# Attention beside a long convolution on one core: the first load in two halves, a filter reversal and a last turn placed later, and VectorE blocks to a later step

## Chip, cores, metric

The kernel runs on one core of one Trainium2 chip. The metric is device time in microseconds (us) of one execution; lower is better. The kernel before took 864.2 us in the median of five runs (860.75, 861.68, 864.2, 867.88, 868.1). The profiled execution took 860.75 us, and its span, from the first to the last instruction, is 859.0 us.

## The reference

Two independent results lie side by side in the output, 512 columns each, for 2048 tokens, all in bf16.

```python
# A: multi-head attention, H = 32 heads of Dh = 16
qkv = (x @ wqkv) -> q, k, v            # x: 2048 x 512
scores = q k^T * Dh ** -0.5            # no mask
a = softmax(scores) v @ wo
# B: short shift, gate, long causal convolution, gate
k_shift[s] = sum_t k[s - 3 + t] * shift_k[:, 3 - t]   # 4 taps a channel
kv = k_shift * v
y = irfft(rfft(kv) * rfft(ssm_k))[:S] + kv * ssm_D    # 2048 taps a channel
b = B_q * y
out = concat([a, b], -1)
```

## The kernel before, in words

**Attention.** The 32 heads are handled four at a time: a block is one head's scores for 128 keys against 512 queries, a 128 x 512 tile in one PSUM bank. There are 4 query quarters x 8 groups x 16 key tiles x 4 heads = 2048 blocks. A group has two passes of four heads; the even and odd heads of a 32-row strip are told apart by two masked copies of the queries, `par` 0 and 1, which VectorE writes as it takes the projected queries out of PSUM (L377, for the first ones L469). Blocks are gathered in steps, `T` = 0 to 740. A step takes two or three banks (`banks_of`, L477 to L484): `emit_qk` issues its score matmuls (L536), ScalarE takes the exponential of the whole step in one instruction (L547), and two steps later `pv_step` and `emit_pv` multiply with the values (L629), accumulating in one bank for the group. At the end of a group VectorE transposes the sums (L693), takes reciprocals (L700), normalises (L704) and transposes back (L715); then the output projection follows (`op_mm`, L746). The last `2 * N_TAIL` blocks go in steps of two, so that the third bank of each set is free for the output projection of the last query quarter (`tail_mm`, `tail_banks`, L1014 to L1019, starting at step NT - 9 = 732).

**VectorE's share of the exponentials.** From step 56 on, `dve_block` may take one block of a three-bank step away from ScalarE. `exp_on_dve` works it out in five VectorE instructions (L583, three of L590, L595). It is allowed when the planned backlog of VectorE is under 3.9 us, and only for T < NT - N_TAIL - GAP = 741 - 9 - 7 = 725 (L557).

**Convolution.** The filter `ssm_k` is loaded as rows (`KZN`), reversed in time by VectorE in four instructions (`kz_turn`, L423), gets `ssm_D` added (`kz_store`, L428), and is stored to a scratch tensor in HBM (L429). From there 512 loads of 512 KB, each a Toeplitz matrix of one channel, stream back through 12 rows of `WR` on SP's queue for the whole run (`load_wr`, L784). `conv_lags` multiplies them with the gated `KV` (L801), with output in the bank `BGB`. After four quads of channels VectorE copies the bank to `YB` (L816); after eight, `conv_turn` transposes `YB` on TensorE (L827) and VectorE multiplies with `B_q` into `QN` (L836). After 64 quads GpSimd's queue stores `QN` to the output.

**What sets the order.** The order is written out when the program is built. A planner keeps a modelled clock for each engine (`Eng.op`, with a duration `us` for each operation) and for the DMAs (`dma`), and places work by it. Each engine then runs its list strictly in order with the semaphore waits that the list implies. VectorE's work that isn't urgent waits in streams (`flow`); `advance` takes from them when the modelled VectorE has time, the stream whose start is earliest first, subject to each piece's `gate`. The four reversals and the store are such pieces (`piece`, L440 to L443), with no gate: they were placed where the model let the filter land. `emit_bg` places the convolution in the room that TensorE has in a step, and the last `conv_turn` as soon as all quads are through (L960 to L963). After it, `keep_busy` issues a spare matmul in each step until 732.

**The start.** SP's queue loads `x` by transposing DMAs, 512 tokens each (`load_x`, L269), then the filter in two halves, `ssm_D`, the rest of `x` and the values of B. ScalarE's queue loads the first 128 columns of the query weights, of the key weights, and then the other weights (L272 to L278). TensorE runs 12 matmuls on zeros (`warm`, L446 to L451), makes the masks (L457), and projects the first queries (L463, 512 tokens in bank 6) and the first 256 keys (L465, bank 7), alternating over the four slices of the contraction. VectorE takes the queries out in two instructions, one for each `par` (L469); ScalarE takes the keys out (L471). Then step 0 begins.

**The end.** `op_mm(qb, 3, 0, 3)` adds three parts of the last output tile; the fourth part of each of the four tiles (L1041) waits for the last group's transposes; VectorE and ScalarE take the tiles out in turn (L766, L764), and SP's and ScalarE's queues store them.

Of the kernel before, what the change touches and what calls it, by code (L numbers as in the profile page):

```python
# [5 lines left out]
ACT = mybir.ActivationFunctionType  # L6
ALU = mybir.AluOpType
# [32 lines left out]
KEYS0 = 256  # L40
# [11 lines left out]
FIX_HI = 2.0 ** 15 - 256.0  # L52
A3, A2, A1 = 255023.64843928182, 77186915383.44943, -6435437372016724.0
A4 = 9.315941845433171e-20
N_TAIL = 9
R_FX = 4
R_EH = 2
R_PTD = 5
T_DVE = 56
T_SLOT = 190  # L60
SLOT = 21
N_SLOT = 25
GAP = 7
AHEAD = 4
BACKLOG = 3.9
MARGIN = 0.35
SPARE = 0.1
# [8 lines left out]
V512 = (0.60, 0.726)  # L76
# [55 lines left out]
def bass_concat_heads__mha_block__ssm_conv_h3__prompt_kernel(  # L132
# [21 lines left out]
    def sem(name):  # L154
        return enter(nc.semaphore(name))
# [5 lines left out]
    xT = sb("xT", [128, 4, S])  # L161
# [30 lines left out]
    WO = WV  # L192
# [16 lines left out]
    def at(*deps):  # L209
        return pe.at(deps)  # L210
# [41 lines left out]
        return dve.op(fn, deps, us=us)  # L252

    d_w = [DmaSem(sem(f"d_w{i}")) for i in range(5)]
    d_x = [DmaSem(sem(f"d_x{i}")) for i in range(4)]
    d_kv = [DmaSem(sem(f"d_kv{i}")) for i in range(6)]
    d_tap, d_kz, d_kzw, d_wo = [DmaSem(sem(n)) for n in ("d_tap", "d_kz", "d_kzw", "d_wo")]
    d_q = [DmaSem(sem(f"d_q{i}")) for i in range(2)]
# [9 lines left out]
    def load_x(sc):  # L268
        h = dma(sp, d_x[sc], xT[:, :, sc * 512:(sc + 1) * 512], x2[sc * 512:(sc + 1) * 512, :], transpose=True)  # L269
        h_x[sc] = [h]  # L270
    load_x(0)
    h_wq = [dma(act, d_w[0], WQ[:, :, 0:128], wview[:, :, 0:128], kb=128)]  # L272
    h_wk = [dma(act, d_w[1], WK[:, :, 0:128], wview[:, :, D:D + 128], kb=128)]
    h_wv = dma(act, d_w[2], WV, wview[:, :, 2 * D:3 * D])
# [142 lines left out]
    def piece(make, deps, us=V512, gate=lambda: True):  # L417
        early_dve.append(("k", deps, make, us, gate))

    def kz_turn(c, us):  # L420
        rev = KZN[c // 2][:, c % 2, :]
        rev = bass.AP(tensor=rev.tensor, offset=KZN[c // 2][:, c % 2, S - 1:S].offset, ap=[rev.ap[0], [-1, S]])
        h_kzt[0] = dve.op(lambda e: e.tensor_copy(KZS[:, c, 0:S], rev), [h_kzl], us=us)  # L423
        if c == 3:
            load_kt(0, h_kzt[0])
# [13 lines left out]

    piece(make_dg, lambda: [], (0.0, 0.0))  # L440
    for c in (2, 3, 0, 1):
        piece(lambda us, c=c: kz_turn(c, us), lambda: [h_kzl])
    piece(kz_store, lambda: [h_kzt[0]], (0.1, 0.22))  # L443


    def warm(e):  # L446
        ins = None
        for _ in range(12):
            ins = e.matmul(PS[:, 0, :], lhsT=PT[:, 0, 0:128], rhs=PT[:, 0, 0:512], start=True, stop=True)
        return ins  # L450
    pe.op(warm, [h_w0], us=(4.0, 4.0))  # L451


    def spread(e):
        ins = None
# [2 lines left out]
        return ins  # L458
    h_mask = pe.op(spread, [h_pat], us=(0.2, 0.3))
    h_mask = bank_free[1] = dve.op(lambda e: e.tensor_scalar(MASK[:, :], PS[:, 1, 0:2], QSCALE, None, ALU.mult), [h_mask])  # L460
    for dc in range(4):
        last_dc = {"start": dc == 0, "stop": dc == 3}
        h = pe.op(lambda e, dc=dc, kw=last_dc: e.matmul(PS[:, 6, :], lhsT=WQ[:, dc, 0:128], rhs=xT[:, dc, 0:512], **kw),  # L463
                  [h_x[0][0], h_wq[0]], us=(0.215, 0.345), run=0.213)
        hk = pe.op(lambda e, dc=dc, kw=last_dc: e.matmul(PS[:, 7, 0:KEYS0], lhsT=WK[:, dc, 0:128], rhs=xT[:, dc, 0:KEYS0], **kw),  # L465
                   [h_x[0][0], h_wk[0]], us=(0.11, 0.24), run=0.107)
    for par in range(2):
        h_q[(0, par)] = bank_free[6] = dve.op(
            lambda e, par=par: e.tensor_scalar(QT[:, 0, par, :], PS[:, 6, :], MASK[:, par:par + 1], None, ALU.mult),  # L469
            [h, h_mask], us=V512)  # L470
    h_k0 = bank_free[7] = act.op(lambda e: e.activation(KTo[:, 0, 0:KEYS0], PS[:, 7, 0:KEYS0], ACT.Copy), [hk], us=(0.28, 0.42))  # L471


    NBLK = NQB * NG * KT * 4
# [79 lines left out]
            exp_on_dve(bl[n], banks[n], h)  # L554

    def dve_block(T):
        if len(banks_of[T]) < 3 or T < T_DVE or T >= NT - N_TAIL - GAP:  # L557
            return None
        i = len(on_dve)
        if i >= R_FX and i - R_FX not in h_last:  # L560
            return None
        todo = sum(us[0] for f in flow for _, _, _, us, _ in f)
        if max(dve.t - pe.t, 0.0) + todo > BACKLOG:
            return None
        n = blk_group(queue[2])
        if len([b for b in queue if blk_group(b) == n]) - 3 >= 2.6 * GAP:
            return queue[2]
        n += 1
        ahead = [b for b in queue if blk_group(b) == n]
        if len(ahead) < 4 * KT - AHEAD + 1 or (n // NG, n % NG) not in h_q or (n % NG // 2, 0) not in h_k:  # L570
            return None
        return ahead[0]
# [166 lines left out]
    def op_mm(qb, t, o0, o1, bank):  # L739
        dd = [bank_free[bank] if o0 == 0 else None, h_wop[0]]  # L740
        dd += [h_otn[(4 * qb + o, t + 1)] if qb == NQB - 1 and o == 3 else h_otn[4 * qb + o] for o in range(o0, o1)]

        def fn(e):
            ins = None
            for o in range(o0, o1):
                ins = e.matmul(PS[:, bank, :], lhsT=OTN[:, (4 * qb + o) % R_O, t * 128:(t + 1) * 128], rhs=WO[:, o, :],  # L746
                               start=(o == 0), stop=(o == 3))
            return ins
        return pe.op(fn, dd, us=(0.105 + 0.215 * (o1 - o0), 0.235 + 0.216 * (o1 - o0)),
                     run=0.213 * (o1 - o0))  # L750
# [70 lines left out]
    def conv_turn(b, bank):  # L821
        pbf = PS[:, bank, :].bitcast(BF16)

        def fn(e):
            ins = None
            for k in range(8):
                ins = e.transpose(pbf[:, 128 * k:128 * k + 128], YB[:, k // 4, 128 * (k % 4):128 * (k % 4) + 128],  # L827
                                  IDN[:, :])
            return ins
        h = pe.op(fn, [bank_free[bank], h_ybw[0], h_idn], us=(0.54, 0.681), run=0.43)  # L830
        h_yb[0] = h
        sl = b // 8
        yv = pbf.rearrange("p (c j) -> p c j", j=32)[:, :, 0:NB].rearrange("p c j -> p j c")
        yv = bass.AP(tensor=yv.tensor, offset=pbf[:, NB - 1:NB].offset, ap=[yv.ap[0], [-1, NB], [32, CHB]])
        qv = QN[:, :, CHB * (b % 8):CHB * (b % 8) + CHB]
        hh = urgent(lambda e: e.tensor_tensor(qv, yv, qv, ALU.mult), [h, h_qn[sl]], slack=0.3, us=V512)  # L836
        bank_free[bank] = hh
        if b % 8 == 7:
            dst = out2[:, D + 256 * sl:D + 256 * (sl + 1)].rearrange("(t p) c -> p t c", p=128)
            ho = dma(pool, d_outB[0], dst, QN[:, :, :], [hh])  # L840
            if sl == 0:
                load_qn(1, [ho])
# [100 lines left out]
    def emit_bg(T):  # L943
        st = state
        unit_step(T)
        if T == N_EARLY:
            assert not early and not part[0]
            load_wop(pe_last())
        if not st["started"] and kv_n[0] == 4:
            st["started"] = True  # L950
        if T in tail_mm:
            assert st["qd"] == C // 4 and not st["turn"], (T, st)
            for t, g in tail_mm[T]:
                op_mm(NQB - 1, t, g, g + 1, tail_banks[t])
            return
        if st["qd"] == C // 4 and not st["turn"] and st["op"] == len(later_op):
            if T < min(tail_mm):
                bank_free[BGB] = pe.op(keep_busy, [bank_free[BGB]])
            return
        if st["turn"] and st["qd"] == C // 4:  # L960
            conv_turn(C // 32 - 1, BGB)
            st["turn"] = False
            return  # L963
        if not st["started"]:
            return
        left_us = max(1.14 * (NT - END - T), 1.0)
        st["lags"] = min(st["lags"] + min(PACE * st["left"] / left_us, RATE) * (pe.t - st["t"]), CAP)
        st["t"] = pe.t
        left = min(LAGS, int(st["lags"]), int((room(T) - 0.06) / 0.055))
        while left > 0 and st["qd"] < wr_next[0] and kv_n[st["qd"] // 32] == 4 and at(h_wr[st["qd"]]) + WAIT <= pe.t:  # L970
            if st["turn"] and st["qd"] % 4 == 3 and st["lag"] + left >= NB:
                left = NB - 1 - st["lag"]
                if left <= 0:
                    break
            n0 = st["lag"]
            if n0 == 0 and st["qd"] % 4 == 0 and at(bank_free[BGB]) > pe.t - 0.2:
                break
            n1 = min(n0 + left, NB)
            left -= n1 - n0
            st["lags"] -= n1 - n0  # L980
            st["left"] -= n1 - n0
            conv_lags(st["qd"], n0, n1)
            st["lag"] = n1 % NB
            if n1 == NB:
                st["qd"] += 1
                if st["qd"] % 4 == 0:
                    st["turn"] = st["turn"] or st["qd"] % 8 == 0
                    break
# [48 lines left out]

    qb = NQB - 1
    op_mm(qb, 3, 0, 3, tail_banks[3])
    for t in range(4):  # L1040
        h = op_mm(qb, t, 3, 4, tail_banks[t])  # L1041
        op_out_end(qb, t, tail_banks[t], h)
# [54 lines left out]
```

## Time and profile before

| what | number |
|---|---|
| median of five runs | 864.2 us |
| profiled execution | 860.75 us |
| its span | 859.0 us |
| ScalarE busy | 837.5 us, 97% |
| VectorE busy | 780.8 us, 91% |
| TensorE busy | 739.2 us, 86% |
| ScalarE's exponentials (L547) | 741 instructions |
| blocks on VectorE (L583) | 212 |
| DMA engines, share of queue q1 | 86.1% |

Read it so: "busy" is time in which the engine has an instruction at work, "idle before" the time that it had none before an instruction of that group, with the instruction or transfer that ended the wait. A time with an `L` is the line of the kernel. A timeline row gives start, duration, engine, line, operation, output and input, count, and in brackets the idle time before it and its releaser; a row of several instructions gives the time from the first's start to the last's end. `SPq` and `ACTq` are the queues on which DMAs are issued, and the duration of such a row is that of the issue, not of the transfer.

### The profile page before, as it was taken

The numbers are of one execution on the slowest core, as the hardware profiler recorded it, in microseconds if no ns is written. First come the engines' busy times: TensorE is split into PE (matmuls) and PEld (weight loads), VectorE is DVE, ScalarE is ACT, GpSimd is POOL, SyncE is SP. The second block draws the span as 40 slices with busy tenths as digits, with TensorE's granted clock in tenths as the row PEclk, the third lists the DMA queues.
The fourth block names the chain that finished last, engine by engine and source line by source line (L and its number), as shares of the span: only waits on it lengthen the run. The fifth ranks groups of instructions, "written<-read, shape, count | busy, mean of one in ns | idle before, by whom it ended". The sixth has DMA issues, their size and how long they took to land.

```text
span 859.0 us, 29408 instructions
## 1 busy us (share of the span) xinstructions
PE 739.2 (86%) x13180; PEld 301.4 (35%) x13180; DVE 780.8 (91%) x1325; ACT 837.5 (97%) x746; POOL 17.3 (2%) x33
## 2 busy tenths in 40 slices
PE   7988999999888888888888888888888888888877
PEld 2222343443333333333333333333333333333332
DVE  3228999999999999999999999999999999999992
ACT  6999999999999999999999999999999999999997
POOL 2000000000000000000000000000000000000000
PEclk9999999999999999999999999999999999999998
DMA  9960059779999999999999999999999999999942
GB/s 271 263 231 2 1 190 334 254 258 320 408 408 407 386 407 393 400 406 404 393 395 376 360 397 388 398 370 397 407 408 394 385 403 409 407 408 393 403 168 71
DMA packets 104813, 289.36 MB, mean 337 GB/s; under 512 B 35184, under 2 KB 37232, under 8 KB 104304
## 3 DMA queue, kind: packets, MB, share of 16 engines
q1 hardware_dynamic: 99424, 279.35, 86.1%
q0 software_dynamic: 1808, 6.29, 2.2%
q10 hardware_dynamic: 3456, 1.84, 0.8%
q8 instruction: 104, 1.70, 0.8%
q14 instruction: 21, 0.17, 0.1%
HBM read 276.83 MB, written 6.42 MB: 330 GB/s over the span
## 4 chain that ended last, share of the span: by engine, by line
ACT 62%; DMA 14%; DVE 12%; PE 7%; SPq 3%; issue 1%; ACTq 0%
ACT PT L547 62%; DMA WR<-kz_scratch 14%; DVE EH L590 5%; PE PS L536 3%; SPq L220 3%; DVE FX L583 2%; DVE PTD L595 2%; PE PS L801 1%; PE PS L629 1%; DMA WR<-in_B_ssm_D_dram 1%; DVE QT L377 1%; PE PS L746 0%; DVE YB L816 0%; DVE DT L693 0%; PE PS L827 0%
## 5 line engine op out<-in xcount | busy, mean ns | idle before, releaser
L547 ACT ACTIVATE PT<-PS 128x1536 bf16<-128x1536 f32 (+1 forms) x741 | 834.5, 1352 | 8.4 <-PE PS L536 7.5
L536 PE MATMUL PS<-QT,KTo 32*128 32x512 bf16 x2048 | 302.2, 385 | 88.4 <-ACT PT L547 72.5
L590 DVE SCALAR_TENSOR_TENSOR EH<-EH,FX 128x512 f32<-128x512 f32 x424 | 283.7, 687 | 0.1
L801 PE MATMUL PS<-WR,KV 128*5 128x128 bf16 (+15 forms) x8192 | 221.7, 220 | 13.6 <-DMA WR<-kz_scratch 12.5
L629 PE MATMUL PS<-PT,VAF 128*32 128x512 bf16 x1836 | 201.1, 391 | 4.6 <-DVE DT L693 2.8
L801 PEld LDWEIGHTS PS<-WR,KV 128*2 128x2 bf16 (+15 forms) x8192 | 148.9, 87 | 96.5 <-issue 37.9
L536 PEld LDWEIGHTS PS<-QT,KTo 32*128 32x128 bf16 x2048 | 72.8, 91 | 266.4 <-ACT PT L547 231.8
L583 DVE TENSOR_SCALAR FX<-PS 128x512 f32<-128x512 f32 x212 | 146.4, 690 | 6.3 <-PE PS L536 5.8
L595 DVE SCALAR_TENSOR_TENSOR PTD<-EH,FX 128x512 uint16<-128x512 f32 x212 | 144.7, 684 | 0.0
L590 DVE SCALAR_TENSOR_TENSOR EH<-FX 128x512 f32<-128x512 uint16 x212 | 144.2, 690 | 0.0
L629 PEld LDWEIGHTS PS<-PT,VAF 128*32 128x32 bf16 x1836 | 48.5, 93 | 119.1 <-issue 105.5
L1007 PE MATMUL PS<-IDN,ZW 128*32 128x512 bf16 (+3 forms) x228 | 71.6, 314 | 0.0
L629 PE MATMUL PS<-PTD,VAF 128*32 128x512 bf16 x212 | 60.0, 385 | 0.0
L402 DVE CAST VAF<-PS 128x512 bf16<-128x512 f32 x16 | 11.1, 692 | 27.9 <-PE PS L360 27.9
L693 DVE STREAM_TRANSPOSE DT<-PS 128x512 f32<-128x512 f32 x31 | 22.3, 718 | 14.5 <-PE PS L629 13.9
L1007 PEld LDWEIGHTS PS<-IDN,ZW 128*32 128x32 bf16 x228 | 21.9, 96 | 11.4 <-issue 10.1
L377 DVE TENSOR_SCALAR QT<-PS,MASK 128x512 bf16<-128x512 f32 x30 | 21.1, 747 | 3.0 <-PE PS L332 2.8
L816 DVE CAST YB<-PS 128x512 bf16<-128x512 f32 x32 | 22.0, 687 | 0.7 <-PE PS L801 0.5
L746 PE MATMUL PS<-WKV,OTN 128*128 128x512 bf16 x64 | 20.6, 400 | 1.2 <-DVE OTN L715 1.2
L360 PE MATMUL PS<-WKV,xT 128*128 128x512 bf16 x64 | 18.8, 384 | 2.8 <-DVE VAF L402 2.2
L341 PE MATMUL PS<-xT,WKV 128*128 128x512 bf16 (+1 forms) x64 | 18.3, 377 | 1.1 <-DVE QT L377 0.5
L332 PE MATMUL PS<-xT,WQ 128*128 128x512 bf16 x60 | 18.2, 384 | 0.1
(64 smaller groups left out, 196.9 us busy)
## 6 DMA issues: line engine op xcount, KB each, us to landing
WR<-kz_scratch SPq DMA_DIRECT2D x512, 512.0 KB, 8.1
kz_scratch<-WR SPq DMA_DIRECT2D x1, 2176.0 KB, 8.5
QN<-in_B_q_dram POOLq DMA_DIRECT2D x2, 1024.0 KB, 12.0
out_dram<-QN POOLq DMA_DIRECT2D x2, 1024.0 KB, 8.1
out_dram<-OUTA POOLq DMA_DIRECT2D x12, 128.0 KB, 5.3
QN<-in_B_ssm_k_dram SPq DMA_DIRECT2D x1, 1024.0 KB, 6.1
QT<-in_B_ssm_k_dram SPq DMA_DIRECT2D x1, 1024.0 KB, 8.0
WR<-in_B_v_dram SPq DMA_DIRECT2D x2, 512.0 KB, 6.5
```

The costliest lines, as they stand in the source:

```text
L220: f(outp, inp).then_inc(dsem.sem, 16)
L377: lambda e, par=par: e.tensor_scalar(QT[:, qb % 2, 2 * o + par, :], PS[:, bank, :], MASK[:, par:par + 1], None, ALU.mult),
L536: ins = e.matmul(PS[:, bank, :], lhsT=KTo[32 * s:32 * s + 32, g // 2, kt * 128:(kt + 1) * 128], rhs=QT[32 * s:32 * s + 32, qb % 2, g, :], ...
L547: h_exp[T] = act.op(lambda e: e.activation(PT[:, T % R_PT, 0:n * QB], PS[:, banks[0]:banks[0] + n, :].rearrange("p b f -> p (b f)"), ACT.E ...
L583: h_f = urgent(lambda e: e.tensor_scalar(fx, PS[:, bank, :], FIX_ADD, FIX_HI, ALU.add, ALU.min), [h, h_last.get(i - R_FX)], slack=0.6)
L590: st["h"] = dve.op(lambda e: e.scalar_tensor_tensor(eh, src, (A3, A2, A1)[j], frac, ALU.add, ALU.mult), [st["h"], h_last.get(i - R_EH), h_ ...
L595: lambda e: e.scalar_tensor_tensor(out16, eh, A4, fx, ALU.mult, ALU.add),
L629: ins = e.matmul(dst, lhsT=w, rhs=rhs, start=(k == 0), stop=(k == KT - 1), tile_position=(0, 32 * s))
L693: h_t = urgent(lambda e: e.transpose(out=dt, in_=PS[:, pvb(n), :]), [h] + before, slack=0.1, us=(0.63, 0.751))
L801: ins = e.matmul(PS[32 * c:32 * c + NB - n, BGB, 128 * (kk % 4):128 * (kk % 4) + 128], lhsT=KV[:, qd, n:NB, c], rhs=WR[:, r + c, 128 * (NB ...
L816: hh = urgent(lambda e: e.tensor_copy(YB[:, half, :].rearrange("p (k i) -> p k i", k=4), src), [h, h_yb[0]], slack=0.3, us=V512)
L1007: pe.op(lambda e: e.matmul(PS[32 * s:32 * s + 32, pvb(n), 0:128 * k], lhsT=ZW[:, :], rhs=rhs, start=False, stop=False, tile_position=(0, 3 ...
```

## The change

`load_x(0)` becomes two transposing loads of 256 tokens. The first 256 keys and first 256 queries are projected from the first, in banks 7 and 6; two warm-up matmuls follow, and the second 256 queries go to bank 5. The queries are taken out in four VectorE instructions of 256 columns in place of two of 512. The first warm-up has 7 matmuls in place of 12. The four filter reversals get a gate: not before the modelled landing of the filter plus 4.0 us. The last `conv_turn` is put off to a later step while the model has the last `YB` copy unfinished, but not past step 731. `N_TAIL` goes from 9 to 7, and the limit of VectorE's blocks from NT - N_TAIL - 7 to NT - N_TAIL - 4, which is 741 - 7 - 4 = 730: the last seven steps then take 2, 2, 2, 2, 2, 2 and 1 blocks, and there are still 741 steps. Ahead of the last four output matmuls, `KEEP` = 4 matmuls with an unused result go to a bank of the last step.

```diff
-N_TAIL = 9
+N_TAIL = 7
+TAIL_GAP = 4
+KZ_LATE = 4.0
+KEEP = 4
...
-    load_x(0)
+    h_x[0] = [dma(sp, d_x[4 * i], xT[:, :, 256 * i:256 * i + 256], x2[256 * i:256 * i + 256, :], transpose=True, kb=256)
+              for i in range(2)]
...
-        piece(lambda us, c=c: kz_turn(c, us), lambda: [h_kzl])
+        piece(lambda us, c=c: kz_turn(c, us), lambda: [h_kzl], gate=lambda: dve.t >= at(h_kzl) + KZ_LATE)
...
-        for _ in range(12):
...
+    warm(7)
...
+    for i in range(2):
+        cols, bank = slice(256 * i, 256 * i + 256), 6 - i
+        for dc in range(4):
+            kw = {"start": dc == 0, "stop": dc == 3}
+            if i == 0:
+                hk = pe.op(lambda e, dc=dc, kw=kw: e.matmul(PS[:, 7, 0:KEYS0], lhsT=WK[:, dc, 0:128], rhs=xT[:, dc, 0:KEYS0], **kw),
+                           [h_x[0][0], h_wk[0]], us=(0.11, 0.24), run=0.107)
+        for dc in range(4):
+            kw = {"start": dc == 0, "stop": dc == 3}
+            h = pe.op(lambda e, dc=dc, kw=kw, cols=cols, bank=bank: e.matmul(PS[:, bank, 0:256], lhsT=WQ[:, dc, 0:128], rhs=xT[:, dc, cols], **kw),
+                      [h_x[0][i], h_wq[0]], us=(0.11, 0.24), run=0.107)
+        if i == 0:
+            h_k0 = bank_free[7] = act.op(lambda e: e.activation(KTo[:, 0, 0:KEYS0], PS[:, 7, 0:KEYS0], ACT.Copy), [hk], us=(0.28, 0.42))
+            warm(2)
+        for par in range(2):
+            h_q[(0, par)] = bank_free[bank] = dve.op(
+                lambda e, par=par, cols=cols, bank=bank: e.tensor_scalar(QT[:, 0, par, cols], PS[:, bank, 0:256], MASK[:, par:par + 1], None, ALU.mult),
+                [h, h_mask], us=(0.335, 0.46))
...
-        if len(banks_of[T]) < 3 or T < T_DVE or T >= NT - N_TAIL - GAP:
+        if len(banks_of[T]) < 3 or T < T_DVE or T >= NT - N_TAIL - TAIL_GAP:
...
         if st["turn"] and st["qd"] == C // 4:
+            if T < min(tail_mm) - 1 and at(h_ybw[0]) > pe.t - 0.2:
+                return
             conv_turn(C // 32 - 1, BGB)
...
     op_mm(qb, 3, 0, 3, tail_banks[3])
+    for i in range(KEEP):
+        pe.op(lambda e: e.matmul(PS[:, banks_of[NT - 1][0], :], lhsT=IDN[:, :], rhs=WO[:, 0, :], start=True, stop=True),
+              [h_exp[NT - 1]], inc=i == KEEP - 1)
```

## Prediction

> **What bounds the kernel now.** I read the page first, then the waits of ScalarE, then the start and the end instruction by instruction.
>
> ```profile
> PE 739.2 (86%) x13180; PEld 301.4 (35%) x13180; DVE 780.8 (91%) x1325; ACT 837.5 (97%) x746; POOL 17.3 (2%) x33
> L547 ACT ACTIVATE PT<-PS 128x1536 bf16<-128x1536 f32 (+1 forms) x741 | 834.5, 1352 | 8.4 <-PE PS L536 7.5
> ```
>
> ScalarE's exponentials are the bound: 834.5 of 859.0 us, with 8.4 us of idle between them. So a change can win only by an earlier first exponential (it starts at 9.64), by fewer of the 8.4 us, by fewer blocks on ScalarE, or by a shorter end (the last one ends near 851.7, 7.3 us before the span does). The groups with shapes kept apart price a block:
>
> ```profile
> L547 ACT ACTIVATE PT<-PS 128x1536 bf16<-128x1536 f32 x354 | 530.3, 1569 | 4.2 <-PE PS L536 3.9
> L547 ACT ACTIVATE PT<-PS 128x1024 bf16<-128x1024 f32 x387 | 411.0, 1155 | 4.1 <-PE PS L536 3.6
> ```
>
> 512 columns more cost 1569 - 1155 = 414 ns. The start, from the issues of the first 2 us and the timeline:
>
> ```profile
> WKV<-in_A_wqkv_dram ACTq DMA_DIRECT2D x1, 128.0 KB, 5.4
> xT<-in_A_x_dram SPq DMA_TRANSPOSE x1, 6.1
> ...
> 1.28 1.08 ACTq L220 DMA_DIRECT2D WKV<-in_A_wqkv_dram  x2
> 1.29 4.11 PE L449 MATMUL PS<-PT 128*128 128x512 bf16 x12 [1.29 <-DVE PT L296]
> ...
> 6.99 0.39 PE L463 MATMUL PS<-xT,WQ 128*128 128x512 bf16 x1 [1.46 <-DMA xT<-in_A_x_dram]
> ...
> 8.40 1.41 DVE L469 TENSOR_SCALAR QT<-PS,MASK 128x512 bf16<-128x512 f32 x2 [2.67 <-PE PS L463]
> ```
>
> The first tokens, issued at 0.81, land at 0.81 + 6.1 = 6.9; the first key weights, issued at 1.28, at 1.28 + 5.4 = 6.7. Both are late, and nearly together. Then the first stall:
>
> ```profile
> 17.87 1.29 DVE L423 COPY WR<-QN 128x2048 bf16<-128x2048 bf16 x2 [2.11 <-DMA WR<-in_B_ssm_D_dram]
> ...
> 20.79 1.02 ACT L547 ACTIVATE PT<-PS 128x1024 bf16<-128x1024 f32 x1 [0.51 <-PE PS L536]
> 21.98 1.45 ACT L547 ACTIVATE PT<-PS 128x1536 bf16<-128x1536 f32 x1 [0.17 <-PE PS L536]
> 23.80 4.66 ACT L547 ACTIVATE PT<-PS 128x1024 bf16<-128x1024 f32 x4 [0.37 <-PE PS L536]
> ```
>
> VectorE stands 2.11 us before the filter reversal, because the filter hasn't landed. The value copy behind it (L402, at 19.08) is late; TensorE's next value projection waits for that copy, and the scores behind it are late for ScalarE. At the end:
>
> ```profile
> 834.86 16.84 ACT L547 ACTIVATE PT<-PS 128x1536 bf16<-128x1536 f32 x15 [0.31 <-PE PS L536]
> ...
> 852.19 0.72 DVE L693 STREAM_TRANSPOSE DT<-PS 128x512 f32<-128x512 f32 x1 [12.51 <-PE PS L629]
> ...
> 854.05 1.89 PE L746 MATMUL PS<-WKV,OTN 128*128 128x512 bf16 x4 [1.16 <-DVE OTN L715]
> ```
>
> VectorE idles for 12.51 us while ScalarE is full; and four matmuls take 1.89 us.
>
> **What the skill says.** The Trainium skill, "TensorE: Matmul & The Clock Gate", section on the HAM clock gate: TensorE runs at half clock until a window of 3413 ns has been busy, falls back after an idle one, and the windows run free of the kernel's start. The trace agrees: granted clock 0.50 in 92.80 to 96.20, in 775.5 to 778.9, and from 853.97, all multiples of 3.41 us from 4.05, where the warm-up matmuls turn fast. It doesn't give the busy share that decides. The windows by stage show TensorE busy for 1.96 us in 4.05 to 7.47, which kept the clock, but 2.67 and 2.31 us before the first two drops and 1.54 us before the last one, so busy time as shown doesn't settle it either. "DMA: Bandwidth & Descriptors", its table of the fixed and variable cost: about 2.0 us of a DMA is fixed, mostly the receipt of the last write. So the second half of a split load need not pay it again behind the first. No run here shows a split.
>
> **The change, part by part**, against the profiled 860.75 us (span 859.0 and 1.75 around it).
>
> *Split load.* The bytes are the same on the same queue, so I put the first half near 5 us (half the stream earlier) and the second at 6.9 as now. But TensorE's new list begins with the key matmuls, and they wait for key weights at 6.7; the query matmuls of both halves are queued behind them. From 6.75: four key matmuls of 256 columns at 0.107 (half of the 0.215 from one 512-column matmul to the next), four query matmuls, two warm-ups of 0.215, four query matmuls: 12 x 0.107 + 0.43 = 1.71, so 8.47, and 0.16 for the last to come through: 8.63. VectorE's 256-column piece takes 0.42 (row of L382 with 256 columns), so the queries are ready at 9.08, against 8.40 + 0.69 = 9.09 now. That is a gain of about **0.1** where early halves look like a microsecond. Bounds: -1.1 if the key weights come by 5.5 (then only four matmuls, 0.6, and 0.42 follow 6.95: 7.97); +1.5 with a cold clock (rival 2). The extra issue on SP moves the filter loads behind it by at most one issue of some 0.5 us; the new gate hides that.
>
> *Warm-up of 7, then 2.* Seven at the cold 0.43 end at 4.3, not 5.4. TensorE is idle until 6.75 anyway, so the matmuls themselves cost nothing. The exposed part is the clock: in 4.05 to 7.47 TensorE would be busy for about 0.25 + 0.2 + 0.7 = 1.2 us in place of 1.96. I take it that the clock stays, since the windows lie differently in each run, and keep the fall as rival 2.
>
> *Filter reversal later.* The stall's ScalarE idle is 0.51 + 0.17 + 0.37 = 1.05. Four copies of 0.65 remain and fall into VectorE's gaps after 23 us, which are 1.1 to 2.3 us each; a copy that delays an urgent one may give some 0.25 back. **-0.8**; bounds -1.2 and +0.3. What follows: the store to the scratch goes out on SP at 34.06, behind a transposing load issued at 27.80, which waits for the first two copies. If all copies are through by 27 nothing moves. If not, SP's later loads shift by as much; the convolution starts only at step 80, near 86 us, so some 40 us cover that.
>
> *Last turn later.* TensorE stood 1.14 us at 833.87 for the `YB` copy, with step 726's scores queued behind it; ScalarE idled 0.31. Put off by a step, the copy is done. **-0.3**; bounds -0.3 and 0. GpSimd's store of `QN`, issued at 835.51 and landing 8.1 later, moves by one step of 1.3 and still ends near 845.
>
> *Blocks to step 729.* 212 blocks over steps 56 to 724 are one in 3.16 steps; five steps more give 1.6. VectorE works them in its 12.51 us of idle (five instructions of 0.69: 3.4 each). 1.6 x 0.414 = **-0.66**; bounds -0.83 (two) and 0 (none). `N_TAIL` leaves 741 steps; it only moves blocks between them: 0. The output parts of 732 to 739 find their banks free as before, since t = 1 starts at 735.
>
> *KEEP.* Four matmuls of 0.215 fill 0.86 of the 1.16 us before 854.05 and end ahead of the transposes. They raise the last window's busy time from 1.54 to 2.4. If the clock stays, the last matmul ends at about 855.05, not 855.94, and ScalarE's last copy gains 0.85. It may not stay: **-0.4**, bounds -0.85 and 0.
>
> Sum: -0.1 - 0.8 - 0.3 - 0.66 - 0.4 = -2.26: 860.75 becomes 858.5. The profiled run was the lowest of five, 3.45 under their median of 864.2, so the median becomes **861.9**, or -0.26%. About 0.5% (4.3 us) is what a measurement of this kernel can tell from no change.
>
> **Rivals.**
>
> 1. *The split pays in full.* The key weights come earlier, two blocks move, the clock holds at the end: -1.1 - 1.2 - 0.3 - 0.83 - 0.85 = -4.3, so **859.9**. For it: every part has its idle time. Against it: key weights at 6.7, with unchanged traffic ahead.
>
> 2. *The clock falls at the start (slower).* If a window ends when its busy time is nearer the 1.2 us worked out above, then 7.47 to 10.9 is cold: the 12 + 2 matmuls take up to 3.4 us in place of 1.7, and the first exponential comes 1.1 to 1.9 later. I take 1.5. A cold window later on cost ScalarE 0.30 + 0.39 (at 94.75 and 96.60), so 0.7 more. The end is cold as now. +1.5 + 0.7 - 0.8 - 0.3 - 0.66 = +0.4: **864.6**, slower than before by a hair. It decides once the start loses more than 1.9 us. For it: 1.2 us is less than any window that kept the clock. Against it: the windows' phase is free.
>
> 3. *The replanned order feeds the convolution worse (slower).* In 215 to 820 TensorE waits 11.8 us, 21 times, for filter rows, and ScalarE's idle there is 4.2. New gates and times change which step each piece of convolution and each VectorE block lands in. If waits double, +4.2 - 2.3 = +1.9: **866.1**. Against it: the queue's own order and bytes don't change.
>
> *That the limit does nothing* is a rival too: if the backlog rule refuses steps 725 to 729, the sum loses 0.66: 862.5, inside the forecast.
>
> **How the numbers follow.** Forecast 0.45 (its own range 858.9 to 864.9), rival 1 0.20, rival 2 0.22, rival 3 0.13. The five runs of before spread over 7.35 us, so a median of a few is itself good to about 2 us. The range runs from rival 1 less 2 to a little over rival 3: 857.5 to 866.5. Faster by over 0.5% is under 859.9: half of rival 1 and a quarter of the forecast, 0.21; slower, over 868.5: a third of rival 3 and a tenth of rival 2, 0.07; the rest, 0.72, is within.
>
> **What would show it.** First exponential near 9.55 (rival 1: 8.5; rival 2: above 10.5, with granted clock 0.5 beside it). No VectorE wait for the filter, and ScalarE's idle before 40 us falling from 2.0 to about 1.2. L583 at 213 or 214. No TensorE wait for `YB` near 833. The four last matmuls 0.2 apart, not 0.43. Wrong would be: a different block count by three or more, or ScalarE's idle in 215 to 820 moving by over 2 us.

## The result, and the profile after

The changed kernel took 870.39 us in the median of 43 runs, the kernel before 867.41 us in the median of 80. The ratio is 1.0039 (95% interval 1.0023 to 1.0055): about 3.4 us slower, where the prediction had 2.3 us faster. A ratio leaves out the runs that took over 1.5% longer than the fastest of their kernel, so it can differ a little from that of the medians. The profiled execution of the changed kernel took 869.75 us. The five runs shown beforehand had a median of 864.2, and the profiled one of them was near the fastest of all 80; so 3.2 us of the distance from the forecast 861.9 lie in the baseline, and the rest in the change. First the page of the changed kernel: ScalarE's busy time and its exponentials, the line now being L559.

```profile
PE 748.3 (86%) x13185; PEld 302.3 (35%) x13185; DVE 784.3 (90%) x1332; ACT 838.2 (97%) x746; POOL 17.3 (2%) x33
L559 ACT ACTIVATE PT<-PS 128x1536 bf16<-128x1536 f32 (+1 forms) x741 | 835.1, 1333 | 19.2 <-PE PS L548 18.3
L595 DVE TENSOR_SCALAR FX<-PS 128x512 f32<-128x512 f32 x213 | 147.2, 691 | 7.9 <-PE PS L548 7.0
```

ScalarE does the same work (835.1 us), but idles 19.2 us before its exponentials, not 8.4; 5.99 of it lie before the first one, against 0.75. VectorE has one more block (213). Two rows of the start of the kernel before, to compare with:

```profile
9.53 0.60 PE L360 MATMUL PS<-WKV,xT 128*128 128x512 bf16 x2
9.64 10.64 ACT L547 ACTIVATE PT<-PS 128x1536 bf16<-128x1536 f32 x9 [0.75 <-PE PS L536]
```

The start, from the timeline of the changed kernel:

```profile
0.81 9.78 SPq L223 DMA_TRANSPOSE xT<-in_A_x_dram  x3
1.27 1.08 ACTq L223 DMA_DIRECT2D WKV<-in_A_wqkv_dram  x2
5.41 1.04 PE L471 MATMUL PS<-xT,WKV 128*128 128x256 bf16 x4 [0.82 <-DMA xT<-in_A_x_dram]
10.58 1.04 PE L475 MATMUL PS<-xT,WQ 128*128 128x256 bf16 x4 [2.43 <-DMA xT<-in_A_x_dram]
12.86 2.52 ACT L559 ACTIVATE PT<-PS 128x1536 bf16<-128x1536 f32 x2 [5.99 <-PE PS L548]
15.87 1.45 ACT L559 ACTIVATE PT<-PS 128x1536 bf16<-128x1536 f32 x1 [0.49 <-PE PS L548]
...
19.74 1.45 ACT L559 ACTIVATE PT<-PS 128x1536 bf16<-128x1536 f32 x1 [1.04 <-PE PS L548]
```

The first half is there at 5.4, and so are the key weights. The second half comes at 10.5, 3.6 us later than the whole load did before, and the first exponential at 12.86, not 9.64. After it, ScalarE stops again and again, where nine exponentials ran on without a stop before. Four matmuls of 256 columns take 1.04 us; at full clock they take 0.61 (in E11 below). So TensorE runs at half its clock here. The end of the changed kernel:

```profile
844.18 0.62 PE L839 MATMUL PS<-IDN,YB 128*128 128x128 bf16 x8
861.61 0.72 DVE L705 STREAM_TRANSPOSE DT<-PS 128x512 f32<-128x512 f32 x1 [9.12 <-PE PS L641]
863.47 1.04 PE L758 MATMUL PS<-WKV,OTN 128*128 128x512 bf16 x4 [0.29 <-DVE OTN L727]
```

That end does what was priced: no wait of TensorE for the last `YB` (1.14 us before), VectorE's idle shorter by one block (9.12 us, not 12.51), and the four matmuls in 1.04 us, not 1.89.

Where the 9.0 us between the two profiled executions lie follows from the start times of the same steps in both traces:

| stretch | before, us | after, us | difference |
|---|---|---|---|
| start to step 0 | 9.64 | 12.86 | +3.22 |
| step 0 to 30 | 35.55 | 39.29 | +3.74 |
| step 30 to 180 | 156.71 | 155.85 | -0.86 |
| step 180 to 724 | 630.27 | 634.30 | +4.03 |
| step 724 to 740 | 18.45 | 18.05 | -0.40 |
| step 740 to the end | 8.41 | 7.67 | -0.74 |

### The profile page after: what moved, and what is told of

Its sections match the earlier page's. It is cut to its first block, busy times and chain, and to the rows that moved or that the text cites. A ratio compares the mean times of both kernels' runs of the same rounds, so it can differ in the third digit from the quotient of the medians.

```text
span 868.0 us, 29430 instructions
## 1 busy us (share of the span) xinstructions
PE 748.3 (86%) x13185; PEld 302.3 (35%) x13185; DVE 784.3 (90%) x1332; ACT 838.2 (97%) x746; POOL 17.3 (2%) x33
## 4 chain that ended last, share of the span: by engine, by line
ACT 58%; DMA 17%; DVE 11%; PE 10%; SPq 2%; issue 1%; ACTq 0%
ACT PT L559 58%; DMA WR<-kz_scratch 16%; DVE EH L602 5%; PE PS L548 4%; SPq L223 2%; PE PS L813 2%; PE PS L641 2%; DVE PTD L607 2%; DVE FX L595 2%; PE PS L364 1%; DMA xT<-in_A_x_dram 1%; DVE QT L381 1%; PE PS L758 1%; DVE DT L705 1%; DVE YB L828 0%
## 5 line engine op out<-in xcount | busy, mean ns | idle before, releaser
L559 ACT ACTIVATE PT<-PS 128x1536 bf16<-128x1536 f32 (+1 forms) x741 | 835.1, 1333 | 19.2 <-PE PS L548 18.3
L1021 PEld LDWEIGHTS PS<-IDN,ZW 128*32 128x32 bf16 x229 | 22.1, 96 | 13.0 <-issue 11.8
L364 PE MATMUL PS<-WKV,xT 128*128 128x512 bf16 x64 | 21.4, 428 | 1.8 <-DVE VAF L406 1.2
```

Source lines behind the costliest of these rows:

```text
L364: return e.matmul(PS[:, bank, :], lhsT=xT[:, dc, kt * 128:(kt + 1) * 128], rhs=WV[:, dc, :], start=(dc == 0), stop=(dc == 3))
L559: h_exp[T] = act.op(lambda e: e.activation(PT[:, T % R_PT, 0:n * QB], PS[:, banks[0]:banks[0] + n, :].rearrange("p b f -> p (b f)"), ACT.E ...
L1021: pe.op(lambda e: e.matmul(PS[32 * s:32 * s + 32, pvb(n), 0:128 * k], lhsT=ZW[:, :], rhs=rhs, start=False, stop=False, tile_position=(0, 3 ...
```

## The experiments

Theory S was that the second half of the load is late and that this sets the loss; theory C that the clock of TensorE at the start does; theory R that the new order starves the convolution. Ratios are to the kernel before, run on the same chip in the same group of runs.

**E1 to E5 and E7: one part undone, or alone.** E1 undoes the split in the changed kernel (`load_x(0)` and the old projection; warm-up of 7).

> The changed kernel with the split undone: one load of 512 tokens, query and key matmuls alternating as in the kernel before; warm-up of 7, late reversal and late end stay. Theory S (the second half of the split load starts only when the first has landed, then shares the DMA engines with the rest of the weights, and so the first exponential comes 3.2 us late): first tokens land near 7.0, first exponential near 9.7, ratio to before about 0.997. Theory C (the short warm-up leaves TensorE at half clock for the start, and that is what costs): first exponential near 10.5, two-matmul value projections of 1.03 us rather than 0.60, ratio about 1.001. Theory R (the replanned order feeds the convolution worse): ScalarE's idle in 215 to 820 stays near 8 us, ratio about 1.002.

E2 is the kernel before with only the split:

```diff
-    load_x(0)
+    h_x[0] = [dma(sp, d_x[4 * i], xT[:, :, 256 * i:256 * i + 256], x2[256 * i:256 * i + 256, :], transpose=True, kb=256)
+              for i in range(2)]
```

> The kernel before with only the split load and its projection in halves; warm-up of 12 and no second warm-up, reversal and end as before. S: the first half lands near 5.4, packets of the second start only after that, it lands near 10.5, the first exponential is near 12.3, ratio 1.004 to 1.006. C: the first exponential near 12 too, but the ratio stays under 1.002 as long as the value projections run at full clock. R: ratio 1.000 to 1.002, and the loss is in 215 to 820.

E5 is the kernel before with `range(7)` for `range(12)` in `warm`:

> The kernel before with 7 warm-up matmuls in place of 12. S: 0 to 0.5 us, ratio 1.000. C: first query matmuls 0.43 apart, first exponential 10.2 to 11.5, ratio 1.002 to 1.004. R: ratio 1.000 unless the modelled times move, which they hardly do here.

E7 is the kernel before with `KZ_LATE`, `N_TAIL = 7`, `TAIL_GAP`, the late last turn and `KEEP`, so without split and with 12 warm-ups:

> The kernel before with the late reversal and the whole late end (N_TAIL 7, limit at step 730, late last turn, KEEP), but with the load in one piece and 12 warm-up matmuls. S and C: the parts that the prediction priced at -0.8, -0.3, -0.66 and -0.4 remain, ratio 0.9975, ScalarE's idle before 40 us near 1.0 after the first exponential at 9.6. R: those gains are lost again in 215 to 820, ratio 1.000 to 1.002.

E3 and E4 are the two halves of E7, the end alone and the reversal alone:

> The kernel before with the late end alone (N_TAIL 7, limit at step 730, late last turn, KEEP). The prediction's terms for it add up to -1.36 us: ratio 0.9984. The last output matmuls stand 0.2 apart, and the span ends 6.9 us after the last exponential, not 7.3. If the 0.9986 of reversal and end together came from the reversal alone, the ratio is 1.000.

> The kernel before with the late filter reversal alone. The prediction's term is -0.8 us, ratio 0.9991: no VectorE wait for the filter, ScalarE's idle before 30 us after the first exponential near 0.3 instead of 1.2 where the clock is full. If the later store of the filter harms the stream of rows, the ratio is over 1.001 and TensorE's wait for rows grows.

| kernel | ratio (95%) | first exponential | step 0 to 30 |
|---|---|---|---|
| E1, split undone | 1.0027 (1.0003 to 1.0051) | 9.92 | 34.53 |
| E2, split alone | 1.0067 (1.0038 to 1.0096) | 14.41 | 39.07 |
| E5, 7 warm-ups alone | 1.0013 (0.9988 to 1.0038) | 10.10 | 43.09 |
| E7, reversal and end | 0.9986 (0.9963 to 1.0009) | 8.94 | 34.53 |
| E3, end alone | 0.9982 (0.9951 to 1.0013) | 9.25* | 38.19* |
| E4, reversal alone | 0.9978 (0.9957 to 0.9999) | 8.63 | 34.53 |

(* E3's trace is of a run that its ratio leaves out, so nothing is read from it.)

The split alone loses 0.67%, the largest effect of any part; S holds, with a first exponential even later than expected. The reversal is a gain by its interval. The end alone isn't shown to be one: its interval holds 1, and the median of all 14 runs is 867.37 us, 1.4 over that of the kernel before. E7's interval excludes neither what S expected (0.9975) nor what R did (1.000). E1 misses what S expected of it (0.997) and has what R expected (1.002); but it differs from E7 in the warm-up of 7 alone, and its ratio is 0.41% higher, where the two intervals, added as squares, allow 0.33%. So the short warm-up costs something too, though E5 by itself doesn't resolve it. From the landing of the first tokens to the first exponential, the traces show 2.7 us in the kernel before, E4 and E7, with 12 warm-ups, but 3.9 and 4.1 in E1 and E5, with 7. What a short warm-up can do after that, E5's trace shows, in TensorE's and ScalarE's timeline:

```profile
9.44 0.61 PE L536 MATMUL PS<-QT,KTo 32*128 32x512 bf16 x3 [0.63 <-DVE QT L469]
9.98 1.03 PE L360 MATMUL PS<-WKV,xT 128*128 128x512 bf16 x2
10.10 2.52 ACT L547 ACTIVATE PT<-PS 128x1536 bf16<-128x1536 f32 x2 [0.87 <-PE PS L536]
...
16.98 1.45 ACT L547 ACTIVATE PT<-PS 128x1536 bf16<-128x1536 f32 x1 [1.04 <-PE PS L536]
```

Two value matmuls take 1.03 us where the kernel before needs 0.60, and ScalarE waits for scores again and again: this trace's clock records begin with full speed only at 34.5 us, and the first 30 steps take 7.5 us longer. In E1, with the same warm-up, the clock came up at 9.6, and steps 0 to 30 took 34.53 as in E7; it lost only the microsecond before step 0. So how long the cold start lasts differs from trace to trace.

**E11: the split, with TensorE kept busy.** `warm(12)` ahead and `warm(14)` between the halves.

> The changed kernel with 12 warm-up matmuls first and 14 in place of 2 between the halves, so that TensorE is hardly idle until the second half lands. Clock theory: the half-rate stretch after the first exponential goes, step 30 comes 34.6 to 35.6 us after step 0 rather than 39.3, and the ratio is near 1.001 though the first exponential is as late as in the changed kernel (12.5 to 14.5). Without an effect of the clock: 39 us again, ratio 1.004 or more.

```profile
10.98 0.61 PE L475 MATMUL PS<-xT,WQ 128*128 128x256 bf16 x4 [1.11 <-DMA xT<-in_A_x_dram]
12.56 0.60 PE L364 MATMUL PS<-WKV,xT 128*128 128x512 bf16 x2
12.61 3.71 ACT L559 ACTIVATE PT<-PS 128x1536 bf16<-128x1536 f32 x3 [5.78 <-PE PS L548]
```

The ratio was 1.0016 (0.9996 to 1.0037). The first exponential is as late as in the changed kernel, but the value matmuls take 0.60 us and steps 0 to 30 take 35.65 us: the clock's part of the loss is gone in this trace, the late half stays. That its ratio is below the changed kernel's 1.0039 isn't clear of the intervals. Against E7's 0.9986 the late half is 0.30%, with an interval of about 0 to 0.6%; that fits the 3.7 us by which the first exponential is later than E7's. The split has a second cost here: the loads behind it are late too. The last part of the filter lands at 19.73, not 17.38 as in E7, VectorE waits 0.96 us for it before the reversal, and steps 0 to 30 take 1.1 us more than E7's 34.53. So what the reversal gained is lost again.

**E14 and E9: more warm-up.** `range(16)`, in the kernel before and in E7.

> The kernel before with 16 warm-up matmuls in place of 12. Clock theory, if the start of the kernel before is itself cold in part of its runs: ratio 0.996 to 0.999. If 12 always suffice: 1.000 to 1.001, from tokens that land before the warm-up ends.

> The load in one piece, late reversal and late end, and 16 warm-up matmuls in place of 12, which reach to the landing of the first tokens. Clock theory: the start is at full clock in more of the runs than with 12, so the ratio falls below the 0.9986 of the same kernel with 12, to 0.995 to 0.998. Without an effect: 0.9986 again, or a little more where the tokens land before the warm-up ends.

E14 gave 0.9998 (0.9974 to 1.0023): no gain over 12 is to be seen in the kernel before, and the expectation of C failed there. E9 gave 0.9955 (0.9921 to 0.9989), median 862.76 us of 11 runs, the best ratio here and faster than the kernel before by its interval. That it beats E7 isn't shown; their intervals overlap, and its trace speaks against it: the tokens land at 6.0, the warm-up runs on to 7.7, and the first exponential comes at 10.40, 1.5 later than E7's.

**E8: why the second half is late.** All weights behind the first two loads wait until it has landed:

```diff
-    h_wv = dma(act, d_w[2], WV, wview[:, :, 2 * D:3 * D])
+    h_wv = dma(act, d_w[2], WV, wview[:, :, 2 * D:3 * D], [h_x[0][1]])
```

> The changed kernel, with the value weights and all that follows them on ScalarE's queue held until the second half of the first tokens has landed. It tells the two causes of the late second half apart. If the second load waits for the first to land and then runs at the full rate (serial start alone), its packets still begin near 5.6 us, but it lands near 7.9. If sharing the DMA engines with the weights is all, its packets begin at 4.0 and it lands near 6.5. If neither counts, it lands near 10.5 as now. The value weights come some 6 us later for it, so the whole may well be slower than the changed kernel: ratio to before 1.002 to 1.008.

The shares of the DMA queues from 4.0 to 5.5 us, q1 being SP's and q10 ScalarE's (a share is of one span of 16 engines; packets overlap). The kernel before:

```profile
q1 hardware_dynamic: 848, 0.21, 69.1%
q10 hardware_dynamic: 421, 0.16, 58.3%
```

The changed kernel:

```profile
q10 hardware_dynamic: 564, 0.37, 105.8%
q1 hardware_dynamic: 38, 0.00, 1.6%
```

E8:

```profile
q1 hardware_dynamic: 1249, 0.30, 100.5%
q10 hardware_dynamic: 129, 0.03, 9.2%
```

In the changed kernel the tokens get almost nothing in that stretch; nearly all goes to ScalarE's queue, where the value weights are. In E8 the second half follows at once and lands 1.0 us after the first. It was issued near 2.2, and its issue line gives 4.1 us to landing, so 6.3; in the changed kernel it is 8.3, so 10.5. The line of E8:

```profile
xT<-in_A_x_dram SPq DMA_TRANSPOSE x1, 4.1
```

The serial start, my first explanation, falls: in E8 the packets run through without a gap. From 5.5 to 10.5 us the second half of the changed kernel is under way, but shares the engines:

```profile
q10 hardware_dynamic: 1099, 0.87, 74.8%
q1 hardware_dynamic: 1239, 0.31, 44.1%
```

The value weights have landed by 7.6; the other weights in this stretch were issued at 2.4 and 3.0, after the second half. So it loses about 1.5 us before it begins, and more by sharing.

E8 as a whole was slower (1.0061, 1.0036 to 1.0086). In its trace the tokens aren't the reason, nor, at first, the late value weights: ScalarE's list has the table load and the copying out of the keys behind the issues that now wait, the last of which holds it from 7.83 to 12.66. The table load starts at 12.69, not 4.36, and the first exponential comes at 15.26:

```profile
12.69 1.28 ACT L313 ACT_TABLE_LOAD   x1 [12.69 <-issue]
```

**E12 and E13: a test that didn't test.** The dummy exponential with its table load was put ahead of the value weights on ScalarE's queue, to delay their issue; E13 also has 12 warm-ups, and none between the halves.

```diff
+    h_j = dve.op(lambda e: e.memset(JNK[:], 0.0))
+    act.op(lambda e: e.activation(JNK[:, 1:2], JNK[:, 0:1], ACT.Exp), [h_j], inc=False)
     h_wv = dma(act, d_w[2], WV, wview[:, :, 2 * D:3 * D])
```

> The changed kernel with one thing moved on ScalarE's queue: the first exponential on a dummy, with its table load of 1.28 us, stands ahead of the issue of the value weights, so that these are issued near 3.4 us, behind the second half of the tokens (issued near 2.2) rather than ahead of it (1.83). Issue-order theory (the second half is late because the 512 KB of value weights were issued before it): its packets follow the first half's at once, it lands near 6.3 to 6.8, the first exponential comes near 8.2 to 8.8, ratio 0.995 to 0.999 with the clock of the start still short of warm-up. Serial start, or a transposing load that gives way to any other: it lands near 10 again, ratio 1.004.

> The same with 12 warm-up matmuls in one go and none between the halves; TensorE then goes from the warm-up straight to the first half's projections. Clock theory: full clock through the start in most runs, first exponential 8.0 to 8.6, step 30 some 34.6 us later, ratio 0.992 to 0.996, the fastest of all kernels here. If the clock counts for nothing the ratio is that of the kernel with 7 and 2.

Ratios 1.0052 (1.0029 to 1.0075) and 1.0080 (1.0056 to 1.0105). The edit didn't move the issue. ScalarE's timeline in E13:

```profile
1.86 1.28 ACT L279 ACT_TABLE_LOAD   x1 [1.86 <-issue]
1.92 0.46 ACTq L223 DMA_DIRECT2D WKV<-in_A_wqkv_dram  x1
```

The weights went out at 1.92 beside the table load, still ahead of the second half, which landed past 10 again. They say nothing on the order of issue, except that it wasn't changed. E13 shows one thing more: 12 warm-ups ahead of the wait for the second half don't keep the clock. It fell to half at 9.3 us, and steps 0 to 30 took 39.25.

**E15 and E16: the issue held back, not the landing waited for.** The value weights wait for the first query weights only (3.3 us); E16 has `warm(12)` and no second warm-up.

```diff
-    h_wv = dma(act, d_w[2], WV, wview[:, :, 2 * D:3 * D])
+    h_wv = dma(act, d_w[2], WV, wview[:, :, 2 * D:3 * D], [h_wq[0]])
```

> The changed kernel, with the issue of the value weights (and of the weights behind them) waiting for the landing of the first query weights, near 3.4 us: after the issue of the second half of the tokens (2.2), but not after its landing. If the order of issue decides: the second half's packets follow the first's at once and it lands near 6.3 to 7, the first exponential comes near 8.2 to 9, ratio 0.996 to 1.001 (the start may be cold with the 7 and 2 warm-up matmuls). If any company slows it: it lands past 9 and the ratio is 1.004 or more.

> The same with 12 warm-up matmuls ahead and none between the halves. If the order of issue decides and the clock counts: first exponential 8.0 to 8.6, step 30 some 34.6 us later, ratio 0.993 to 0.997. If the order of issue doesn't decide: first exponential past 12, ratio 1.004 or more. If the clock doesn't count: the ratio of the kernel with 7 and 2.

E15's DMA queues from 4.0 to 5.5 us, and the issue line of its second half:

```profile
q1 hardware_dynamic: 1012, 0.25, 102.8%
q10 hardware_dynamic: 122, 0.03, 19.9%
...
xT<-in_A_x_dram SPq DMA_TRANSPOSE x1, 4.4
```

The second half lands at 6.6, with the value weights issued and waiting since 3.3 (the weights behind them on that queue go later too). So the order of issue decides here which of the two is served first; sharing with weights issued later, as in the changed kernel after 5.5 us, still stretches a load. E15's ratio is 0.9989 (0.9967 to 1.0012), clear of the changed kernel's 1.0039 (1.0023 to 1.0055): one line that changes the order takes the loss away. E16's is 0.9973 (0.9950 to 0.9996). Both start later than expected. E15's first exponential comes at 10.32, with TensorE's projections at half speed (1.03 and 1.06 us for four matmuls). E16's comes at 9.35, and then ScalarE stops for 2.05 us at 16.0:

```profile
9.35 4.62 ACT L558 ACTIVATE PT<-PS 128x1536 bf16<-128x1536 f32 x4 [1.82 <-PE PS L547]
16.02 8.45 ACT L558 ACTIVATE PT<-PS 128x1536 bf16<-128x1536 f32 x7 [2.05 <-PE PS L547]
```

In E16 the clock records give half speed from 13.0 to 16.4, and four value matmuls take 1.89 us there, against 1.04 at 11.2; the tokens that follow land at 14.6, later than the 12.4 of before. What would avoid that stop wasn't tried. So a split that works as meant shows no gain here: its second half lands at 6.7, and in the traces of E1, E4, E5, E7, E9 and E14, with an undivided load, all 512 tokens land between 5.9 and 6.3 (6.95 in the kernel before was the latest of the seven). E4 and E7, undivided and with 12 warm-ups, have their first exponential at 8.63 and 8.94, ahead of E16's.

## Why the prediction was wrong, point by point

**Split load: the step that failed.** The prediction said "the bytes are the same on the same queue" and put the second half "at 6.9 as now". The bytes were the same, but not the place in line. An issue of a transposing load takes 1.36 us for 256 tokens and 1.42 for 512, not "some 0.5 us", so halving saves nothing, and the second half goes out at 2.2, behind the 512 KB of value weights issued at 1.83 on the other queue. In the kernel before all 512 tokens were ahead of them. The term was -0.1 with bounds -1.1 and +1.5; the first exponential measured +3.2 in the changed kernel, and the split alone 0.67%. E15 shows that the place in line is the cause. I had read the DMA rows for landings and not for the order of issue across the two queues, which the same timeline shows. The other half of that step, key weights at 6.7 holding the first half, didn't come true either: they landed at 5.1. That gain is swallowed by the wait for the second half. Both landings, 6.9 and 6.7, came from one trace, the latest of these seven with an undivided load; in the others the key weights landed at 5.4 to 6.0. The sum itself doesn't close either: 8.63 + 0.42 is 9.05, not 9.08, which is 0.04 below 9.09, not 0.1.

**Warm-up: rival 2's mechanism, with another size.** I took it that the clock stays. In the changed kernel the clock records give full speed only from 26.8 us. Rival 2 priced that at 1.1 to 1.9 on the first exponential and 0.7 after it. The first price was good: E1 and E5 lose 1.2 and 1.4 between landing and first exponential. The second was far too small: step 0 to 30 took 3.74 longer here, and 7.5 in E5, because the cold stretch lasts: 17.1 us from 10.2 in E2, five times the 3.41 of the one window that rival 2 took as cold at the start. (The gains that it set against the start are 1.76 by its own terms, not 1.9.) Here two edits meet: the short warm-up costs by itself, and the wait for the second half alone is enough, since E2 with 12 warm-ups, where TensorE waits 4.41 us for it, fell back to half clock and took 39.07. The traces of the changed kernel, E2, E12 and E13 all start cold after that wait; E11, which fills it, doesn't.

**Filter reversal:** right. The trace of E4 has steps 0 to 30 in 34.53, 1.0 less than before, against 0.8 foreseen; VectorE's copies moved to 20.2 to 23.3 without a wait. That the gate hides a later filter failed with the split, as E11's wait of 0.96 us shows. The ratio, 0.9978, is -1.9 us with an interval from about 0 to -3.7.

**Last turn, blocks, KEEP:** right in kind. One block moved, not 1.6, so -0.41 in place of -0.66: it starts at 847.46 in the changed kernel. The 0.31 of ScalarE's idle at the last turn is gone, and step 724 to 740 is 0.40 shorter. The last stretch from step 740 to the end is 0.74 shorter, of which the shorter last step has a part. The traces with KEEP end 6.9 us after the last exponential. Without it two of the single-part traces ended 7.3 after it and two 6.9, so the gain of 0.44 comes where the clock would have fallen.

**Rival 3** isn't borne out, though the sign named for it came: ScalarE's idle in 215 to 820 moved by over 2 us. Steps 180 to 724 took 4.03 longer than in the profile of before, TensorE's waits for filter rows in 215 to 820 grew from 11.8 to 16.2, and ScalarE's idle from 4.2 to 7.8. But E5 and E14, which change only the number of warm-ups, show an idle of 7.8 as well. And from step 180 to 724 the order of ScalarE's and VectorE's instructions is the same in all traces: the replanning didn't reach there. Over fifteen traces (all but E3's) this stretch ranges from 630.3 to 637.8 with a median of 633.5; that of before was the shortest of all, and the changed kernel is 0.8 over the median. The 4 us are the luck of the trace that I built the sum on.

**The sum.** Reversal and end give -1.2 us by E7 (its interval holds 0), the late half about +3, and the clock, as an estimate, makes up the rest in some of the runs. E2's +5.8 holds the late half and its cold start together. A finer division between the two within the 3.4 us isn't settled: the cold start comes in a part of the runs, and there is one trace of each kernel.

## What to carry to other kernels

Before splitting a load, list the issues of all queues in order of time and see what comes between the halves: here a half issued behind another queue's large transfer began only after it, however early its own first half was. A wait near the start that left TensorE idle cost twice here, because the work behind it needed the full clock; so price the cold stretch to its end and not as one window. Compare a landing time over several traces before building on it. And take the sum from a profiled run only after asking where that run stands among the others; here it was at the fast edge of a spread of 20 us.

## What the runs showed of the hardware that was not expected

- The stretch from step 180 to 724 in the same fifteen traces goes with the time that the clock records put at half speed in it: between 0 and 27.3 us, with a correlation of 0.87, and a straight line of 630.4 us + 0.23 us for each us at half clock. The order of the work there is the same in all, so a good part of the spread between runs of one kernel may be the clock. The Trainium skill, "TensorE: Matmul & The Clock Gate", Part 1 on the HAM clock gate, says that the windows run free of the kernel. That fits: the first half-clock stretch after step 180 starts at 775.5 us in the kernel before and at 489.6 in E14, which has the same work there. That the windows cause the spread was only read from this correlation.
- The same part also tells that the ramp penalty, the cost of the cold start, is less than 1% of a typical span. Here it is: 3.7 to 7.5 us of 860. But that is as much as a whole set of edits is worth.
- The clock column of the windows view reads 1.00 in 0 to 4.05 of the kernel before, while the warm-up matmuls there stand 0.43 apart: before the first clock record it tells nothing. The spacing of the matmuls does.
- The issue of a DMA on ScalarE's queue doesn't wait for a table load that stands ahead of it in the program (1.92 against 1.86 in E13).
